# Alternating the two tokens of an output block over its partitions: x's columns reordered, stores from every other partition

## The chip, the cores and the metric

The kernel runs on one core of a Trainium2 chip. The metric is the device time of one execution in microseconds (us), and less is better. Before the change the median of three runs is 231.18 us (231.02 to 231.35).

## What is computed

The reference is a linear attention whose output goes through a feed-forward network with a multiplicative gate. There are 8 batches, 8 heads, 576 tokens in each batch and 64 channels in each head; the network goes from 512 to 1024 to 512 channels. q, k, v, the weights and the output are float32.

```python
def _attn_ref(q, k, v):
    q_s = exp(q - max(q, over channels));  q_s = q_s / (sum(q_s, over channels) + 1e-09)
    k_s = exp(k - max(k, over tokens));    k_s = k_s / (sum(k_s, over tokens) + 1e-09)
    kv = einsum('bhsd,bhse->bhde', k_s, v)
    return einsum('bhsd,bhde->bhse', q_s, kv)

def _moe_ref(x, w1, w2, w3, w_out):
    a = x @ w1
    b = x @ w2
    h = a * b @ w3
    return h @ w_out

x = attn_out.transpose(0, 2, 1, 3).reshape(B * S, H * D)     # 4608 tokens x 512
out = _moe_ref(x, w1, w2, w3, w_out)
```

## The kernel before, in words

**Weights.** `w3` and `w_out` are multiplied once, at the start, into one matrix `W3O`, so that the network is a gate (two products with `w1` and `w2`, multiplied element by element into `ab`) and one product of `ab` with `W3O`.

**Tokens.** A batch is one chunk. A token s of a batch is written as s = 9p + j, with p from 0 to 63 and j from 0 to 8. The attention of a batch gives x transposed, with channels on partitions and tokens along the columns. The tile `x` (128 partitions, 4 blocks of channels, 512 columns, f16) holds the tokens with j from 0 to 7, in the order j first, p second, so the 64 tokens of one j are neighbours. The tokens with j = 8 of all batches go into a tile of their own, `xtail`, which is a ninth chunk at the end.

**From attention to x.** The matmuls `xm` (line 704) write the attention's output into PSUM; `xs` evicts it with a factor into `x`, on ACT (line 369) or DVE (line 371). Batches 0 and 1 are split: their first 256 columns (`xs.b.0.i`) and their second 256 columns (`xs.b.1.i`) are evicted apart, each eviction writing two of the four blocks of channels, i = 0 the blocks 0 and 2, i = 1 the blocks 1 and 3. In the other batches an eviction writes all 512 columns of one block. There are 32 such evictions, 26 on ACT and 6 on DVE.

**The gate.** In batches 0 to 5, `up` (line 850) multiplies x with `w2` and `w1` into the PSUM tiles `pab`; the first product is evicted as `bsb`, and DVE multiplies the second with it into `ab` (line 865). In a split batch one `up` has 8 matmuls: two groups of 128 gate channels, in each the four blocks of channels of 256 columns. Chunks 6 to 8 make their gate from sums of x's halves of 256 columns (lines 921 and 938).

**The output.** In chunks 0 and 1, `down` (line 872) gives a block of 128 tokens and all 512 output channels. In chunks 2 to 8 seven products (line 1028) give blocks with 2 times 128 tokens and 256 output channels. A block's partitions are 128 neighbouring columns of x: partitions 0 to 63 hold the tokens of one j, partitions 64 to 127 those of the next j. Each block of chunks 0 to 7 is stored by two DMAs from SP's queue, one for each half of the partitions (lines 912 and 1071). That makes 64 issues, 56 that read `osb` and 8 that read `k` and `v`, input buffers that chunk 7 uses again. The ninth chunk is stored from all 128 partitions (lines 1058 and 1064).

**The order.** Each engine's order is written out by hand in the table `ORDER` at the top of the file. SP's queue holds the stores, most loads of q, k and v, and the transposing DMAs (line 679), which turn `en` (the softmax of q) into `qT`. The engines run in the order given and wait on semaphores; the waits are put in by the tile framework, from the regions of tiles that the instructions write and read.

The beginning of the first chunk, which the prediction speaks of, stands so in the table:

```python
... xm.0.0 pf.6.0 pf.6.1 xs.0.0.1 kmx.1.0 xs.0.0.0 xm.0.1 xs.0.1.0 xs.0.1.1 up.1.0.0.0 bs.0.0.0 xt.0 ...
```

So on PE the first product of the gate (`up.1.0.0.0`, which reads columns 0 to 255 of x) follows the matmuls `xm.0.1`, whose eviction writes columns 256 to 511; after it come the matmuls `xt` for the ninth chunk.

Of the kernel before, what the change touches and what calls it, by code (L numbers as in the profile page):

```python
# [265 lines left out]
def kernel(  # L266
# [12 lines left out]
    B, H, S, D = q.shape  # L279
# [7 lines left out]
    HALF = P // G  # L287
    HH = H // G
    NHP = HH // 2
    NJ = S // HALF  # L290
# [4 lines left out]
    SC = 2.0 ** 4.5  # L295
# [29 lines left out]
    st = {}  # L325
# [41 lines left out]
    def scale(eng, out, in_, by):  # L367
        if eng == "ACT":
            nc.scalar.mul(out=out, in_=in_, mul=by)
        else:  # L370
            engine[eng].tensor_scalar_mul(out=out, in0=in_, scalar1=by)
# [148 lines left out]
    def attention(b):  # L520
# [119 lines left out]
        def qeps(p, eng):  # L640
            rr = st["qr", b][:, :, slice(*PARTS[p])]
            if eng == "ACT":
                nc.scalar.activation(out=rr, in_=rr, func=AF.Identity, bias=epst[:, 0:1])
            else:
                return [dve.tensor_scalar_add(out=rr, in0=rr, scalar1=EPS)]
# [40 lines left out]
        def xtile():  # L686
            if ("x", b) not in st:
                st["x", b] = work.tile([P, N_CT, MAIN], F16, tag="x", name="x", bufs=NX)
            return st["x", b]
# [18 lines left out]
                            rhs=toks(i, hp, gg, j0, j1), start=True, stop=True)  # L708

        def xs(name, i, dst, eng):  # L710
            scale(eng, dst(), st[(*name, i)], SC)

        A0 = LEAD[min(b, 2)]

# [19 lines left out]
        for p in parts:  # L734
            n = (PARTS[p][1] - PARTS[p][0]) * HH * D
# [6 lines left out]
              lambda eng, p=p: qeps(p, eng), [("qsm", b, p)])  # L742
# [24 lines left out]
        if len(SUBS[b]) == 2:  # L767
            for h in range(2):
                name = ("xm", b, h)
                dst = lambda i, h=h: xtile()[:, i::2, h * 256:(h + 1) * 256]  # L770
                A(name, "PE", 0.22, lambda name=name, h=h: prod(name, [0, 1], 4 * h, 4 * h + 4, None),
                  kvs + qready(h) + free, takes=XRING(name), slots=2, slack=SLACK)
                for i in range(2):
                    A(("xs", b, h, i), moves(512), 0,
                      lambda eng, name=name, i=i, dst=dst: xs(name, i, lambda: dst(i), eng), [name],
# [3 lines left out]
        else:  # L779
            for hp in hps:  # L780
                name = ("xm", b, hp)
                A(name, "PE", 0.22, lambda name=name, hp=hp: prod(name, [hp], 0, NM, None),
                  kvs + qready(0) + qready(1) + free, takes=XRING(name), slots=2, slack=SLACK)
                for i in range(2):
                    A(("xs", b, hp, i), moves(512), 0,
                      lambda eng, name=name, i=i, hp=hp: xs(
                          name, i, lambda: xtile()[:, 2 * hp + i:2 * hp + i + 1, :], eng),
# [5 lines left out]
        for i in range(2):  # L793
            A(("xts", b, i), moves(128), 0,
              lambda eng, i=i: xs(("xt", b), i, lambda: xtail[:, i::2, b * HALF:(b + 1) * HALF], eng),
              [("xt", b)], gives=[("xt", b)])
# [39 lines left out]
    def chunk(c):  # L836
# [68 lines left out]
        def os2(tb, c0, c1, eng):  # L905
            st["osb", c, tb, c0] = obuf(c1 - c0)
            copy(eng, st["osb", c, tb, c0], st["po", c, tb, c0][:, 0:c1 - c0])

        def store(tb):
            for i in range(2):  # L910
                b, j = c, 2 * tb + i
                nc.sync.dma_start(
                    out=out[b * S:(b + 1) * S, :].rearrange("(p j) c -> p j c", j=NJ)[:, j, :],
                    in_=st["osb", c, tb][i * HALF:(i + 1) * HALF, :])

        def x_sum(i, eng):
            x0, x1 = [x()[:, 0:2, t:t + 256] for t in (0, 256)], [x()[:, 2:4, t:t + 256] for t in (0, 256)]
            b11, b12, b21, b22 = x0[0], x0[1], x1[0], x1[1]
            s = xsums(c)
            in0, in1 = {1: (b12, b11), 2: (b22, s[0]), 3: (b22, b12), 4: (b21, s[1])}[i]  # L920
            return [engine[eng].tensor_tensor(out=s[i - 1], in0=in0, in1=in1, op=ALU.subtract)]
# [79 lines left out]
        def sums_of(i, eng):  # L1001
            a = st["ab", c]
            a11, a12, a21, a22 = [a[:, 4 * f:4 * f + 4, 256 * t:256 * t + 256]
                                  for t in range(2) for f in range(2)]
            in0, in1, op = {1: (a21, a22, ALU.add), 2: (mine[0], a11, ALU.subtract),
                            3: (a11, a21, ALU.subtract), 4: (a12, mine[1], ALU.subtract)}[i]
            return [engine[eng].tensor_tensor(out=mine[i - 1], in0=in0, in1=in1, op=op)]  # L1007
# [47 lines left out]
        def store_block(n, part=None):  # L1055
            t0, c0 = n // 10 - 1, (n % 10 - 1) * 256
            if part is not None:
                (nc.sync if part else nc.scalar).dma_start(
                    out=out.rearrange("(t p j) c -> p t j c", p=P, j=NJ)[
                        :, 2 * t0 + part, NM, c0:c0 + 256],  # L1060
                    in_=st["osb", c, n][:, 256 * part:256 * part + 256])
                return
            if c == B:
                nc.sync.dma_start(
                    out=out.rearrange("(t p j) c -> p t j c", p=P, j=NJ)[
                        :, 2 * t0:2 * t0 + 2, NM, c0:c0 + 256],
                    in_=st["osb", c, n].rearrange("p (t x) -> p t x", t=2))
                return
            for i in range(2):
                j = 4 * t0 + i  # L1070
                nc.sync.dma_start(
                    out=out[c * S:(c + 1) * S, :].rearrange("(p j) c -> p j c", j=NJ)[
                        :, j:j + 3:2, c0:c0 + 256],
                    in_=st["osb", c, n][i * HALF:(i + 1) * HALF, :].rearrange(
                        "p (t x) -> p t x", t=2))

        A = plan.add
        nf = len(SUBS[c])
# [7 lines left out]
        if c in UPS + UP1:  # L1086
# [15 lines left out]
            for i, needs in ((1, []), (2, [("xd", c, 1)]), (3, []), (4, [("xd", c, 2)])):  # L1102
                A(("xd", c, i), {"POOL": (1.06, True), "DVE": (0.39, True)}, 0,
                  lambda eng, i=i: x_sum(i, eng), needs + xn + held)
            for g in range(2):
                for one in kinds:
                    k = lambda i: ("vk", one, c, g, i)
                    p = lambda i: ("vp", one, c, g, i)
# [12 lines left out]
                    for n, needs, gives in (  # L1121
# [8 lines left out]
                        b = ("bs", c, sub, u)  # L1130
# [33 lines left out]
        if c in SEVEN:  # L1164
# [8 lines left out]
            for i, needs in ((3, lo), (1, lo + hi), (2, [("sa", c, 1)]), (4, [("sa", c, 2)])):  # L1173
                A(("sa", c, i), {"POOL": (1.9, True), "DVE": (0.69, True)}, 0,
                  lambda eng, i=i: sums_of(i, eng), needs + last)
# [39 lines left out]
        for sub in range(nf):  # L1215
            for tb in range(4):
# [18 lines left out]
                for c0, c1 in zip(cuts, cuts[1:]):  # L1235
# [4 lines left out]
                      lambda eng, tb=tb, c0=c0, c1=c1: os2(tb, c0, c1, eng), [("down", *it)] + gone,  # L1240
# [6 lines left out]
    def weight_sum(i, eng):  # L1247
        b11, b12, b21, b22 = [W3O[:, 4 * f:4 * f + 4, 256 * x:256 * x + 256]
                              for f in range(2) for x in range(2)]
        in0, in1 = {1: (b12, b11), 2: (b22, sums[0]), 3: (b22, b12), 4: (b21, sums[1])}[i]  # L1250
        return [engine[eng].tensor_tensor(out=sums[i - 1], in0=in0, in1=in1, op=ALU.subtract)]

    for i, needs in ((1, []), (2, [("sT", 1)]), (3, []), (4, [("sT", 2)])):
        plan.add(("sT", i), {"POOL": (1.9, True), "DVE": (0.69, True)}, 0,
                 lambda eng, i=i: weight_sum(i, eng),
# [48 lines left out]
```

## Time and profile before

| What | us |
|---|---|
| median of 3 runs | 231.18 (231.02 to 231.35) |
| the profiled execution's own time | 230.82 |
| its span, first to last instruction | 229.0 |
| PE busy | 221.0 (96% of the span) |
| DVE busy | 202.4 (88%) |
| ACT busy | 146.2 (64%) |
| POOL busy | 144.0 (63%) |

The profile shows one execution. In a row of an engine's timeline stand the start and the length in us, the engine, the line, the operation, the tiles as written <- read, the shapes, the number of instructions merged into the row, and in brackets how long the engine was idle before it and who ended that. Matmuls are pipelined, and a row of them reaches past the moment at which the next row's first matmul starts; the distance between two rows' starts tells what a group took. SP only issues DMAs.

### The profile page before, as it was taken

Reading aid. Unit: us, or ns where it says so; the run is one execution under the profiler, and the core shown is the slowest. Engines: PE = TensorE matmul, PEld = TensorE weight load, DVE = VectorE, ACT = ScalarE, POOL = GpSimd, SP = SyncE. Lnnn points to the kernel's source line nnn. Section 1 sums busy time; section 2 is a strip of 40 time slices with the busy share of each in tenths; the row PEclk is TensorE's granted clock in tenths of the full one; section 3 lists DMA queues with packets and bytes.
Section 4 is the critical chain, followed back from the end, with each engine's and each line's share of the span. In section 5 each row is a group of like instructions: output and inputs, shape, how many; then the busy total and the mean of one; then the engine's idle time right before and its main releaser. Section 6 shows DMA issues by size and latency. Waiting matters only on the chain.

```text
span 229.0 us, 5580 instructions
## 1 busy us (share of the span) xinstructions
PE 221.0 (96%) x2239; PEld 149.3 (65%) x2239; DVE 202.4 (88%) x313; ACT 146.2 (64%) x277; POOL 144.0 (63%) x93
## 2 busy tenths in 40 slices
PE   7889999999999999999999999999999999999993
PEld 2445658865857644345666665664788788888882
DVE  2996769989896999999999899899989999899982
ACT  1536855479963999959947988448568453344531
POOL 8233347919999997984895894643199335628200
PEclk9999999999999999999999999999999999999999
DMA  6999999999999889999792867972804430041437
GB/s 202 218 308 215 291 264 258 316 383 305 399 306 239 345 274 216 294 277 339 229 394 63 166 137 170 345 144 53 178 1 88 95 64 1 3 92 35 106 90 231
DMA packets 42201, 46.56 MB, mean 203 GB/s; under 512 B 17088, under 2 KB 29888, under 8 KB 42176
## 3 DMA queue, kind: packets, MB, share of 16 engines
q1 hardware_dynamic: 34496, 34.35, 53.8%
q0 software_dynamic: 7536, 11.73, 21.9%
q8 instruction: 17, 0.28, 0.5%
q10 hardware_dynamic: 144, 0.13, 0.2%
q14 instruction: 8, 0.07, 0.1%
HBM read 38.80 MB, written 9.44 MB: 211 GB/s over the span
## 4 chain that ended last, share of the span: by engine, by line
PE 73%; POOL 9%; DMA 9%; issue 4%; DVE 3%; ACT 1%; POOLq 0%; DVEq 0%
PE pab L850 27%; PE po L1028 16%; PE pg L938 9%; PE pab L938 7%; DMA w<-in_moe_w_dram 7%; PE po L500 4%; POOL k L554 3%; PE pab L1028 2%; POOL en L656 2%; DMA qT<-en 2%; PE pkv L579 2%; POOL q L624 2%; PE po L872 2%; PE xm L704 1%; PE w3t L488 1%
## 5 line engine op out<-in xcount | busy, mean ns | idle before, releaser
L850 PE MATMUL pab<-x,w1sb 128*128 128x256 f16 (+1 forms) x256 | 49.5, 326 | 0.2 <-DMA w1sb<-in_moe_w_dram 0.2
L850 PE MATMUL pab<-x,w2sb 128*128 128x256 f16 (+1 forms) x256 | 49.5, 326 | 0.0
L554 POOL TENSOR_TENSOR k<-k,cb 128x1152 f32<-128x1152 f32 x13 | 34.1, 2631 | 14.4 <-DVE w L1007 8.6
L850 PEld LDWEIGHTS <-w1sb 128*128 128x128 f16 x256 | 24.6, 98 | 14.9 <-DMA w1sb<-in_moe_w_dram 0.5
L850 PEld LDWEIGHTS <-w2sb 128*128 128x128 f16 x256 | 24.3, 98 | 15.1 <-issue 1.1
L865 DVE TENSOR_TENSOR ab<-pab,bsb 128x512 f16<-128x512 f32 x48 | 31.8, 676 | 1.9 <-ACT bsb L365 1.2
L624 POOL TENSOR_TENSOR q<-q,qm 128x1280 f32<-128x1280 f32 (+1 forms) x13 | 27.8, 2142 | 4.7 <-issue 2.3
L365 ACT CAST bsb<-pab 128x512 f16<-128x512 f32 x37 | 21.7, 586 | 12.6 <-PE pab L850 12.1
L656 POOL TENSOR_TENSOR en<-eq,qr 128x1024 f16<-128x1024 f16 (+1 forms) x12 | 25.4, 2123 | 6.0 <-ACT bsb L365 5.0
L619 DVE TENSOR_REDUCE qm<-q 128x20 f32<-128x1280 f32 (+1 forms) x16 | 21.3, 1339 | 3.5 <-DMA q<-in_q_dram 3.5
L637 DVE TENSOR_REDUCE qr<-eq 128x20 f32<-128x1280 f16 (+1 forms) x16 | 21.4, 1340 | 1.1 <-ACT eq L632 1.0
L632 ACT ACTIVATE eq<-q 128x1280 f16<-128x1280 f32 (+1 forms) x16 | 18.6, 1168 | 5.4 <-DVE q L624 3.8
L1028 PEld LDWEIGHTS <-w 128*128 128x128 f16 x192 | 18.6, 98 | 4.1 <-issue 0.4
L531 DVE TRANSPOSE_TENSOR_REDUCE kt<-k 128x72 f32<-128x2304 f32 x8 | 20.6, 2570 | 0.3 <-DMA k<-in_k_dram 0.3
L365 ACT COPY q<-pg 128x512 f32<-128x512 f32 x19 | 10.9, 586 | 13.9 <-PE pg L938 7.7
L1028 PEld LDWEIGHTS <-ab 128*128 128x128 f16 x168 | 16.4, 98 | 3.5 <-issue 0.2
L562 ACT ACTIVATE ek<-k 128x1152 f16<-128x1152 f32 x16 | 18.4, 1166 | 0.0
L1028 PE MATMUL po<-w 128*128 128x256 f16 x144 | 18.0, 273 | 0.0
L1007 POOL TENSOR_TENSOR w<-ab 128x1024 f16<-128x1024 f16 x5 | 10.6, 2126 | 9.7 <-DVE ab L993 3.7
L500 PE MATMUL po<-wosb,w3T 128*128 128x512 f16 x64 | 15.3, 379 | 0.6 <-DMA wosb<-in_moe_w_out_dram 0.5
L872 PE MATMUL po<-W3O,ab 128*128 128x512 f16 x64 | 15.1, 379 | 0.0
L365 ACT CAST v<-v 128x1152 f16<-128x1152 f32 x12 | 13.6, 1156 | 1.2 <-DMA v<-in_v_dram 1.1
(145 smaller groups left out, 426.0 us busy)
## 6 DMA issues: line engine op xcount, KB each, us to landing
out_dram<-osb SPq DMA_DIRECT2D x56, 128.0 KB, 2.5
q<-in_q_dram SPq DMA_DIRECT2D x5, 1152.0 KB, 8.2
v<-in_v_dram SPq DMA_DIRECT2D x5, 1152.0 KB, 7.1
k<-in_k_dram SPq DMA_DIRECT2D x4, 1152.0 KB, 9.5
k<-in_k_dram POOLq DMA_DIRECT2D x3, 1152.0 KB, 14.1
v<-in_v_dram POOLq DMA_DIRECT2D x1, 1152.0 KB, 13.6
q<-in_q_dram SPq DMA_DIRECT2D x2, 576.0 KB, 5.7
k<-in_k_dram SPq DMA_DIRECT2D x2, 576.0 KB, 5.7
```

Source lines behind the costliest of these rows:

```text
L365: return [(nc.scalar.copy if eng == "ACT" else engine[eng].tensor_copy)(out=out, in_=in_)]
L500: nc.tensor.matmul(st["pf", ft], lhsT=st["w3T", ft][:, gt, :], rhs=wosb[:, gt, :], start=(gt == 0), stop=(gt == N_FT - 1))
L531: dve.tensor_reduce(out=st["kt", b].rearrange("p h j e -> p (h j e)"), in_=kb.rearrange("p h j (e c) -> p (h j e) c", c=QD), axis=AX.X, op ...
L554: return [engine[eng].tensor_tensor(out=kb[:, two(hp), :, :], in0=kb[:, two(hp), :, :], in1=st["cb", b][:, two(hp), None, :].broadcast_to( ...
L619: dve.tensor_reduce(out=st["qm", b][:, :, j], in_=qb[:, :, j, :], axis=AX.X, op=ALU.max)
L624: return [engine[eng].tensor_tensor(out=qb[:, :, j, :], in0=qb[:, :, j, :], in1=st["qm", b][:, :, j, None].broadcast_to([P, HH, n, D]), op ...
L637: dve.tensor_reduce(out=st["qr", b][:, :, slice(*PARTS[p])], in_=st["eq", b, p], axis=AX.X, op=ALU.add)
L656: return [engine[eng].tensor_tensor(out=st["en", b][:, j, :, :].rearrange("p j h d -> p h j d"), in0=st["eq", b, p], in1=st["qr", b][:, :, ...
L850: nc.tensor.matmul(st["p", one, c, sub, u][:, a * (t1 - t0):(a + 1) * (t1 - t0)], lhsT=w[:, ct, fb * P:(fb + 1) * P], rhs=x()[:, ct, t0:t1 ...
L865: dve.tensor_tensor(out=st["ab", c][:, nf * u:nf * u + nf, t0:t1], in0=cut(st["p", 0, c, sub, u]), in1=cut(st["bsb", c, sub, u]), op=ALU.mult)
L938: nc.tensor.matmul(st["pg", one, c, g, bank][:, a * 256:a * 256 + 256], lhsT=t[:, c0 + ct, f:f + P], rhs=r[:, r0 + ct, t0:t0 + 256], start ...
L1028: nc.tensor.matmul(to, lhsT=t[:, f0 + ft, t0 + tb * P:t0 + tb * P + P], rhs=r[:, g0 + ft, c0:c0 + 256], start=fresh and (tb == 0 or wide_) ...
```

## The change

`xs` writes the evicted columns in another order. In each run of 256 columns, which are four values of j, let j = 2z + t within the run; the column of token (p, j) was 128z + 64t + p and is now 128t + 2p + z. An output block (128 columns, one t) then holds the tokens of two values of j alternately, z = 0 on the even partitions and z = 1 on the odd ones. The two stores of a block take the even and the odd partitions, 64 each, where they took the lower and the upper half; in chunks 2 to 7 the two rows of the output that one partition's data goes to are now neighbours (j and j + 1), where they were j and j + 2. The `xtail` tile and the ninth chunk's stores are left as they are. Each store moves as many bytes as before, and no instruction is added or removed.

```diff
         def xs(name, i, dst, eng):
-            scale(eng, dst(), st[(*name, i)], SC)
+            to, ps = dst(), st[(*name, i)]
+            if name[0] == "xm":
+                if ps.shape[1] == 1:
+                    to = to[:, 0, :].rearrange("p (a t c z) -> p a z t c", t=2, z=2, c=HALF)
+                    ps = ps[:, 0, :].rearrange("p (a z t c) -> p a z t c", t=2, z=2, c=HALF)
+                else:
+                    to = to.rearrange("p a (t c z) -> p a z t c", z=2, c=HALF)
+                    ps = ps.rearrange("p a (z t c) -> p a z t c", z=2, c=HALF)
+            scale(eng, to, ps, SC)
...
         def store(tb):
-            for i in range(2):
-                b, j = c, 2 * tb + i
+            for z in range(2):
+                j = tb // 2 * 4 + tb % 2 + 2 * z
                 nc.sync.dma_start(
-                    out=out[b * S:(b + 1) * S, :].rearrange("(p j) c -> p j c", j=NJ)[:, j, :],
-                    in_=st["osb", c, tb][i * HALF:(i + 1) * HALF, :])
+                    out=out[c * S:(c + 1) * S, :].rearrange("(p j) c -> p j c", j=NJ)[:, j, :],
+                    in_=st["osb", c, tb][z::2, :])
...
-            for i in range(2):
-                j = 4 * t0 + i
+            for z in range(2):
+                j = 4 * t0 + 2 * z
                 nc.sync.dma_start(
                     out=out[c * S:(c + 1) * S, :].rearrange("(p j) c -> p j c", j=NJ)[
-                        :, j:j + 3:2, c0:c0 + 256],
-                    in_=st["osb", c, n][i * HALF:(i + 1) * HALF, :].rearrange(
-                        "p (t x) -> p t x", t=2))
+                        :, j:j + 2, c0:c0 + 256],
+                    in_=st["osb", c, n][z::2, :].rearrange("p (t x) -> p t x", t=2))
```

Below is what the built programs show at the beginning of the first chunk. On PE before, from the last matmul of `xm.0.1` over the first product of the gate (8 weight loads and 8 matmuls, the first pair shown) to the matmuls `xt`; a name in brackets is the semaphore of an engine, or of a DMA queue, that the instruction waits for:

```order
L704 MATMUL xm<-qT,kv_479 64x256
L850 LDWEIGHTS w2sb [waits DMASW3_49]
L850 MATMUL pab<-x,w2sb 128x256
...
L704 LDWEIGHTS kv_479
L704 MATMUL xt<-qT,kv_479 64x64 [waits Activation_49]
L704 LDWEIGHTS kv_479
L704 MATMUL xt<-qT,kv_479 64x64
L704 LDWEIGHTS kv_479
L704 MATMUL xt<-qT,kv_479 64x64 [waits DVE_49]
```

The same place on PE in the changed kernel, the first three pairs of the gate's product shown (line 858 is line 850 before):

```order
L704 MATMUL xm<-qT,kv_479 64x256
L858 LDWEIGHTS w2sb [waits DMASW3_49]
L858 MATMUL pab<-x,w2sb 128x256
L858 LDWEIGHTS w2sb
L858 MATMUL pab<-x,w2sb 128x256 [waits Activation_49]
L858 LDWEIGHTS w2sb
L858 MATMUL pab<-x,w2sb 128x256 [waits DVE_49]
...
L704 LDWEIGHTS kv_479
L704 MATMUL xt<-qT,kv_479 64x64 [waits PE_49]
```

The instructions stand in the same order, but the waits for ACT and for DVE have moved ahead, from the first and third matmul of `xt` to the second and third matmul of the gate's first product. They wait for the same two counts as before, those of the evictions `xs.0.1.0` on ACT and `xs.0.1.1` on DVE. This is the only place in the program at which an instruction waits for something else than before.

On DVE, at the eviction `xs.0.1.1` before:

```order
L531 TENSOR_REDUCE kt<-k_1_76 128x72 [waits DMASW2_49]
L371 TENSOR_SCALAR x<-xm 128x2x256 [waits PE_49]
L619 TENSOR_REDUCE qm<-q_1_78 128x4x4 [waits DMASW4_49]
L537 TENSOR_REDUCE mx<-kt 128x8 [waits DVE_49]
L371 TENSOR_SCALAR W3O<-po 128x512
```

The same in the changed kernel:

```order
L531 TENSOR_REDUCE kt<-k_1_76 128x72 [waits DMASW2_49]
L371 TENSOR_SCALAR x<-xm 128x2x2x128 [waits PE_49]
L619 TENSOR_REDUCE qm<-q_1_78 128x4x4 [waits DMASW4_49]
L537 TENSOR_REDUCE mx<-kt 128x8 [waits DVE_49]
L371 TENSOR_SCALAR W3O<-po 128x512
```

The eviction keeps its place, its wait and its 512 elements; its output pattern has one more dimension (two blocks, two values of z, 128 columns at a distance of two). The other evictions of x, on DVE and on ACT, change in the same way, and nothing else on these engines, on POOL or in SP's queue differs in place or in what it waits for.

## The prediction

> **What bounds the kernel now.** I read the page's busy times and the chain of waits first, then PE's waits, then the timelines around the places that the change touches.
>
> ```profile
> span 229.0 us, 5580 instructions
> PE 221.0 (96%) x2239; PEld 149.3 (65%) x2239; DVE 202.4 (88%) x313; ACT 146.2 (64%) x277; POOL 144.0 (63%) x93
> PE 73%; POOL 9%; DMA 9%; issue 4%; DVE 3%; ACT 1%; POOLq 0%; DVEq 0%
> ...
> PE xm L704 <- DMA qT<-en: 0.4, 1, 0.4
> PE pab L850 <- DMA w1sb<-in_moe_w_dram: 0.2, 1, 0.2
> PE po L1028 <- ACT x L369: 0.2, 1, 0.2
> ```
>
> PE is busy for 221.0 of 229.0 us, and these three rows are all the waits that its matmuls have behind the weights' folding. So nearly every us by which PE's stream is held up is paid, unless it meets one of these waits, and hardly anything can be won on another engine or on a DMA. The chain goes through POOL and a transposing DMA up to 73 us, and from there through PE to the end, with one eviction of x in it:
>
> ```profile
> 68.20 4.95 DMA qT<-en
> 73.15 0.14 issue
> 73.28 0.41 PE xm L704 x4
> ...
> 181.36 0.56 ACT x L369
> 181.92 0.04 issue
> 181.96 1.03 PE po L1028 x8
> ```
>
> **The change, part by part.** It touches three things: a wait on PE, the write pattern of 32 evictions, and the source pattern of 64 stores.
>
> *The wait.* PE and the two evictions at the first chunk:
>
> ```profile
> 33.57 1.05 PE L850 MATMUL pab<-x,w2sb 128*128 128x256 f16 x8
> 34.55 0.25 PE L704 MATMUL xt<-qT,kv 64*64 64x64 f16 x8
> ...
> 35.67 1.04 PE L850 MATMUL pab<-x,w2sb 128*128 128x256 f16 x8
> 36.54 1.04 PE L850 MATMUL pab<-x,w1sb 128*128 128x256 f16 x8
> 33.68 0.60 ACT L369 ACTIVATE x<-xm 128x512 f16<-128x512 f32 x1 [1.07 <-PE xm L704]
> 33.72 0.69 DVE L371 TENSOR_SCALAR x<-xm 128x512 f16<-128x512 f32 x1 [0.28 <-PE xm L704]
> ```
>
> Before, the gate's first product starts at 33.57, beside the evictions of `xm.0.1`, since it reads only the other half of the columns. In the changed program its second matmul waits for ACT and its third for DVE. The reason is in the pattern: the eviction with i = 0 writes blocks 0 and 2 with a stride, and taken as one run from its first to its last element it also covers block 1's first half, which the second matmul reads; the one with i = 1 covers block 2's first half, which the third reads. The data don't ask for it. A group of 8 matmuls takes 36.54 - 35.67 = 0.87 us, 0.109 each, so the third starts at 33.57 + 0.22 = 33.79 now. It will start when DVE ends, 33.72 + 0.69 = 34.41, and 0.04 later (the issue row at 181.92, PE behind an eviction of x): 34.45. ACT ends at 34.28, which is earlier. The stall is 34.45 - 33.79 = **0.66 us**. Everything on PE behind it, `xt` first, is late by that; `xt`'s own waits for the same two engines were met at 34.55 and are gone, which at most gives the hundredths that they may have cost.
>
> *What takes it back.* The next places at which PE waits for something that doesn't depend on PE:
>
> ```profile
> 44.40 1.04 PE L850 MATMUL pab<-x,w2sb 128*128 128x256 f16 x8
> 45.63 1.05 PE L850 MATMUL pab<-x,w1sb 128*128 128x256 f16 x8 [0.19 <-DMA w1sb<-in_moe_w_dram]
> 47.39 1.89 PE L872 MATMUL po<-W3O,ab 128*128 128x512 f16 x8
> ...
> 49.31 0.69 DVE L365 COPY osb<-po 128x512 f32<-128x512 f32 x1 [0.69 <-PE po L872]
> 49.92 1.35 DVE L554 TENSOR_TENSOR k<-k,cb 128x1152 f32<-128x1152 f32 x1
> 51.35 2.64 POOL L554 TENSOR_TENSOR k<-k,cb 128x1152 f32<-128x1152 f32 x1 [5.00 <-DVE k L554]
> 53.95 6.51 POOL L624 TENSOR_TENSOR q<-q,qm 128x1280 f32<-128x1280 f32 x3
> 60.40 1.15 POOL L365 CAST v<-v 128x1152 f16<-128x1152 f32 x1
> 61.67 6.50 POOL L656 TENSOR_TENSOR en<-eq,qr 128x1280 f16<-128x1280 f16 x3
> ```
>
> The group at 45.63 would have started at 44.40 + 0.87 = 45.27, had its weights been there. It lost 0.36; the weights' load was issued long before 33 us and doesn't move. With 0.66 of delay the group is ready at 45.93 and waits no more: 0.66 - 0.36 = **0.30 us** is left. This delay goes on along two ways. PE itself is late by 0.30. And DVE's copy at 49.31 waits for PE's product of 47.39, DVE's subtraction at 49.92 stands behind it in DVE's order, and POOL's at 51.35 waits 5.00 us for that; from there POOL's queue has no gap to the `en` that ends at 61.67 + 6.50 = 68.17, so the transposing DMA is issued 0.30 later as well.
>
> ```profile
> 71.83 1.04 PE L850 MATMUL pab<-x,w1sb 128*128 128x256 f16 x8
> 73.28 0.41 PE L704 MATMUL xm<-qT,kv 64*64 64x512 f16 x4 [0.41 <-DMA qT<-en]
> ...
> 60.00:70.00 10.00, 10.00 (x157) 6.80 (x156) 9.90 (x16) 6.82 (x14) 9.87 (x6) 1.00 1.02 330
> qT<-en SPq DMA_TRANSPOSE x13, 3.8
> ```
>
> The two ways meet at 73.28. Before, PE's last group ends at 72.87 and PE waits 0.41 for `qT`. PE's own 0.30 fits into that. So what counts is by how much `qT` lands later: by 0.30 if its transfer takes its 4.95 again, by nothing if the transfer was held by the DMA engines' queue rather than by its issue. The queue is full (a DMA share of 1.02 between 60 and 70 us), and 4.95 is 1.15 over the median of 3.8, which would cover the 0.30; but SP issues in order, and the loads that compete move back with the transposes. I take **0.2 us** between the ends 0 and 0.30, nearer the upper since most of what stands around the transfer moves with it. From 73.28 the chain is PE's alone, so the 0.2 stays to the end. Price of the wait: +0.2, with bounds 0 (all absorbed) and 0.66 (nothing absorbed).
>
> *The evictions.* 26 on ACT and 6 on DVE now write f16 at a distance of two elements. The number of elements stays. No row of this kernel has such a write.
>
> ```profile
> L369 ACT ACTIVATE x<-xm x18: 577/597/632, 31.5 to 181.8; 128x512 f16<-128x512 f32 x18
> L371 DVE TENSOR_SCALAR x<-xm x4: 679/686/692, 33.7 to 182.1; 128x512 f16<-128x512 f32 x4
> L365 ACT COPY osb<-po x10: 583/586/592, 52.2 to 180.5; 128x512 f32<-128x512 f32 x10
> ```
>
> ACT takes 597 ns for 512 f16 elements side by side and 586 ns for 512 f32: twice the bytes at the same time, so the price goes by elements and not by how closely they lie. DVE's 686 ns for 512 is likewise over 1 ns an element. I take 0. The upper end is that a scattered element costs double, +0.6 us an eviction. PE covers most of them with other work; not covered are the one of 33.7 us and the pair before PE's wait at 181.96, so at that end the kernel loses up to 0.6 + 2 x 0.6 = 1.8 us. The lower end is 0.
>
> The Trainium skill (SBUF — State Buffer, "Door 1: The DMA port swizzle") says that an engine's strided access keeps its full rate while at least two accesses fall into one 16-byte line; f16 at a distance of two has four, so by this rule the price is 0 too. No run here shows it yet.
>
> *The stores.*
>
> ```profile
> L1071 SPq DMA_DIRECT2D out_dram<-osb x40: 595/603/652, 123.7 to 211.6; - x40
> L912 SPq DMA_DIRECT2D out_dram<-osb x16: 502/582/1927, 51.3 to 113.1; - x16
> L1058 SPq DMA_DIRECT2D out_dram<-v x1: 344/344/344, 225.7 to 225.7; - x1
> out_dram<-osb SPq DMA_DIRECT2D x56, 128.0 KB, 2.5
> out_dram<-v SPq DMA_DIRECT2D x2, 256.0 KB, 2.6
> ```
>
> 64 stores keep their bytes, their pieces and their place in SP's queue. An issue takes 582 to 603 ns; I bound it by the shortest and longest rows, 344 and 1927, and take no change. Behind the stores in SP's order stand loads and transposes; the only one of these on the chain is that of 68.20 us, and the four stores ahead of it are issued by 55.1 us, so even the long issue would be hidden there. The landing may get shorter: a store of 256 KB from all 128 partitions lands in 2.6 us, one of 128 KB from 64 neighbouring partitions in 2.5, so 64 neighbours move about half as fast. No wait of a computing engine names an output store, so I cost this at nothing; its cover is the ring of four `osb` buffers. At the program's end the last stores are the ninth chunk's, which don't change.
>
> The Trainium skill (same page and section) gives this as a rule: partitions 0 to 63 reach 8 of the 16 ports between SBUF and the DMA engines, and only a range with both halves reaches all. The two rows agree with it. By the rule the changed stores would be faster, and a kernel bound by stores would win; that is the third rival below.
>
> **The sum.** 0.66 - 0.36 - 0.10 = +0.2 us. Against the profiled execution's 230.82 (1.82 more than its span) that is 231.0; the median of the runs, 231.18, stands 0.36 above that execution, so I forecast 231.18 + 0.2 = **231.4 us**, less than 0.2% (0.46 us) above, which is about what a measurement of this kernel can tell from no change.
>
> **The rivals.**
> - *The stall is paid in full: slower.* PE's 0.66 is taken back only where the weights at 45.63 and `qT` at 73.28 come at the same time as before. If the loads at these two places come later by chance or because the DMA engines' order shifts, 0.5 to 0.7 stays: 231.7 to 231.9. It decides from 0.46 us that are not absorbed. For it: PE has no other gap of that size up to 181 us. Against it: the load of w1 was issued before the stall.
> - *The scattered writes are slower.* From +0.15 us an eviction the three uncovered ones and the stall at 33.7 together pass 0.46; at double price 231.18 + 0.2 + 1.8 = 233.2. Against it: 597 and 586 ns for f16 and f32.
> - *The stores give the DMA engines time back.* Four stores of 51.3 to 55.1 us lie ahead of the loads that `qT` waits behind. If these are done sooner, `qT` lands sooner, but PE is ready only at 72.87 + 0.30, so at most about 0.1 is won against 73.28: 231.1. To be faster by over 0.2% more than this is needed, for instance 0.2 at the end of the program.
> - *Nothing happens:* the added waits are met when PE comes to them. Against it: DVE ends its eviction 0.62 us after PE's third matmul starts.
>
> **How the numbers follow.** Forecast (0 to 0.45 left): 0.50, all of it within 0.2%. Full stall: 0.20, slower. Slower writes: 0.12, slower. Stores: 0.13, of which 0.10 faster, with something besides, and 0.03 within. Nothing: 0.05, within. So faster 0.10, within 0.2% 0.58, slower 0.32. The range must leave out no more than 0.2: below, the stores' case is cut at 230.7, which leaves out about 0.07; above, 232.2 takes in the full stall and the writes at half the upper end, and leaves out about 0.07. The likeliest case alone is 231.2 to 231.6.
>
> **What will show it.** In the changed kernel PE should wait for DVE's x inside the first gate product near 34.4 us, and start `xt` about 0.66 later; the wait for w1 at 45.63 should be gone, and that for `qT` at 73.28 small. The 32 evictions should keep 597 and 686 ns, and the stores of chunks 2 to 7 should land in less than 2.5 us with no engine gaining. I am wrong if a gap appears on PE behind 73 us, if an eviction of x is longer by over 0.1 us, or if an issue of a store on SP grows so that a transpose comes late.

## The result and the profile after

The changed kernel takes 231.59 us (median of 17 runs, 231.26 to 231.81), the kernel before 231.01 us beside it (17 runs, 230.67 to 231.40). The ratio is 1.0022, with a 95% interval of 1.0015 to 1.0029: slower by 0.58 us. The ratios here and below are taken over all runs of both kernels, so they can differ by up to 0.1% from the quotient of two medians. The profiled execution of the changed kernel took 231.59 us, its span is 229.8 us against 229.0.

All waits of PE's matmuls behind the folding of the weights, after (us in total, times, longest); of before three such rows stand in the prediction:

```profile
PE pab L858 <- ACT x L369: 0.6, 1, 0.6
PE xm L704 <- DMA qT<-en: 0.5, 1, 0.5
...
PE po L1036 <- ACT x L369: 0.3, 1, 0.3
```

The first is the moved wait. The wait for w1 is gone, the one for `qT` is there as before, and the last is longer by 0.1. The chain of waits now goes through the added wait, and then, as before, through the transposing DMA:

```profile
33.90 0.73 ACT x L369
34.63 0.04 issue
34.67 0.93 PE pab L858 x7
...
68.77 4.94 DMA qT<-en
73.71 0.14 issue
73.85 0.41 PE xm L704 x4
```

The evictions of x by tile and form (ns as minimum, median and maximum, then first and last start), after:

```profile
L369 ACT ACTIVATE x<-xm x18: 725/744/779, 31.7 to 182.7; 128x512 f16<-128x512 f32 x18
...
L369 ACT ACTIVATE x<-po x8: 738/747/775, 96.2 to 182.1; 128x512 f16<-128x512 f32 x8
L371 DVE TENSOR_SCALAR x<-xm x4: 711/726/731, 33.9 to 183.0; 128x512 f16<-128x512 f32 x4
...
L371 DVE TENSOR_SCALAR x<-po x2: 728/728/728, 139.3 to 182.4; 128x512 f16<-128x512 f32 x2
```

On ACT an eviction went from 597 to 744 ns (+0.15 us), on DVE from 686 to 726 (+0.04). The stores' issue on SP, after, in the same form:

```profile
L1079 SPq DMA_DIRECT2D out_dram<-osb x40: 600/604/720, 124.9 to 212.5; - x40
```

The DMA part of the profile after: packets, MB and share of the 16 engines' time of the queue that the stores are in, and the median landing of the stores in us:

```profile
q1 hardware_dynamic: 34496, 34.35, 49.8%
...
out_dram<-osb SPq DMA_DIRECT2D x56, 128.0 KB, 2.2
```

The queue's row before:

```profile
q1 hardware_dynamic: 34496, 34.35, 53.8%
```

An issue takes what it took (604 ns, before 603). A store of 128 KB lands in 2.2 us instead of 2.5, and the same 34.35 MB occupy the DMA engines for 4 points less. This is what the Trainium skill says (SBUF — State Buffer, "Door 1: The DMA port swizzle") of partitions spread over both halves.

**Where PE loses the time.** PE's timeline after, at the places of the prediction (start, length, and in brackets the idle time ahead):

```profile
33.78 0.28 PE L858 MATMUL pab<-x,w2sb 128*128 128x256 f16 x1
34.67 0.93 PE L858 MATMUL pab<-x,w2sb 128*128 128x256 f16 x7 [0.61 <-ACT x L369]
35.53 0.26 PE L704 MATMUL xt<-qT,kv 64*64 64x64 f16 x8
...
36.60 1.04 PE L858 MATMUL pab<-x,w2sb 128*128 128x256 f16 x8
...
46.20 1.04 PE L858 MATMUL pab<-x,w1sb 128*128 128x256 f16 x8
47.08 1.04 PE L858 MATMUL pab<-x,w2sb 128*128 128x256 f16 x8
...
73.85 0.41 PE L704 MATMUL xm<-qT,kv 64*64 64x512 f16 x4 [0.53 <-DMA qT<-en]
...
81.59 1.03 PE L858 MATMUL pab<-x,w2sb 128*128 128x512 f16 x4
82.65 1.67 PE L880 MATMUL po<-W3O,ab 128*128 128x512 f16 x7
...
182.91 1.03 PE L1036 MATMUL po<-W3O,ab 128*128 128x256 f16 x8 [0.31 <-ACT x L369]
```

and before, where the prediction didn't show it:

```profile
81.03 1.03 PE L850 MATMUL pab<-x,w2sb 128*128 128x512 f16 x4
81.89 1.89 PE L872 MATMUL po<-W3O,ab 128*128 128x512 f16 x8
```

The gate's first product starts at 33.78 (before 33.57): this execution is 0.21 late already, from the load of the first weights, and that has nothing to do with the change. Counted from there, the product of 36.60 (before 35.67) is 0.72 late, that of 47.08 (46.52) 0.35, `xm` at 73.85 (73.28) 0.36, the output's product at 82.65 (81.89) 0.55 and that of 182.91 (181.96) 0.74; the end of the span is late by 0.8 - 0.21 = 0.59. This agrees with the 0.58 us between the medians. So there are three losses (the wait, one near 82 us, one near 182 us), one return at the w1 wait, and 0.15 that come back between 182 us and the end. Of these, 0.06 come back at once: the group at 182.91 takes 0.87 us to the next group's start, where it took 0.93 before. The rest lies behind the last store, further below.

The second loss is ACT's. Its timeline before:

```profile
75.94 1.09 ACT L369 ACTIVATE x<-xm 128x512 f16<-128x512 f32 x2
...
81.18 0.58 ACT L365 COPY osb<-po 128x512 f32<-128x512 f32 x1
```

and after:

```profile
76.50 1.36 ACT L369 ACTIVATE x<-xm 128x512 f16<-128x512 f32 x2
...
82.01 0.58 ACT L365 COPY osb<-po 128x512 f32<-128x512 f32 x1
```

Two evictions took 1.09 us and take 1.36. From there to the copy of `osb` ACT has no gap in either. The copy empties the PSUM tile that PE's next `po` product writes. Before, it ended at 81.76, and PE came to the product at 81.89, 81.89 - 81.03 = 0.86 us after its last group's start: a reserve of 0.13 us. Now PE would come at 81.59 + 0.86 = 82.45, but the copy ends at 82.59 and PE starts at 82.65: about 0.2 us are lost.

### The profile page after: what moved, and what is told of

It is laid out like the page before. It is cut to its first block, busy times and chain, and to the rows that moved or that the text cites. A ratio compares the mean times of both kernels' runs of the same rounds, so it can differ in the third digit from the quotient of the medians.

```text
span 229.8 us, 5580 instructions
## 1 busy us (share of the span) xinstructions
PE 220.6 (96%) x2239; PEld 149.2 (65%) x2239; DVE 202.6 (88%) x313; ACT 149.1 (65%) x277; POOL 144.1 (63%) x93
## 3 DMA queue, kind: packets, MB, share of 16 engines
q1 hardware_dynamic: 34496, 34.35, 49.8%
## 4 chain that ended last, share of the span: by engine, by line
PE 82%; DMA 9%; POOL 4%; DVE 2%; ACT 1%; issue 1%; DVEq 0%; POOLq 0%
PE pab L858 33%; PE po L1036 16%; PE pg L946 9%; PE pab L946 7%; DMA w<-in_moe_w_dram 7%; PE po L880 5%; PE po L500 4%; PE pab L1036 2%; PE pkv L579 2%; DMA qT<-en 2%; POOL en L656 2%; PE xm L704 1%; PE w3t L488 1%; POOL w L449 1%; ACT x L369 1%
## 5 line engine op out<-in xcount | busy, mean ns | idle before, releaser
L369 ACT ACTIVATE x<-xm 128x512 f16<-128x512 f32 x18 | 12.7, 748 | 3.6 <-PE xm L704 3.6
```

## The experiments

A table from PE's timelines comes first, since most of the verdicts rest on it; it has all runs but the one in which the matmuls themselves reorder the columns: times in us between five landmarks, which are the start of the gate's first product, the start of its second `w2` product, `xm` behind the `qT` wait, the output's product near 82 us, the one near 182 us behind ACT's x, and the end of the span. For before they are 33.57, 35.67, 73.28, 81.89, 181.96 and 229.0. Where a kernel ran in two groups of runs, both values stand.

| kernel | first product to second | to `xm` | to 82 us | to 182 us | to the end | ratio [95%] |
|---|---|---|---|---|---|---|
| before | 2.10 | 37.61 | 8.61 | 100.07 | 47.0 | 1 |
| after | 2.82, 2.81 | 37.25, 37.14 | 8.80, 8.80 | 100.26, 100.26 | 46.9, 46.9 | 1.0022 [1.0015, 1.0029], 1.0017 [1.0005, 1.0029] |
| stores only | 2.05, 2.05 | 37.22, 37.43 | 8.61, 8.61 | 100.30, 100.26 | 46.9, 47.0 | 0.9984 [0.9973, 0.9996], 0.9993 [0.9978, 1.0009] |
| order only | 2.82, 2.82 | 37.20, 37.16 | 8.80, 8.79 | 100.45, 100.31 | 47.0, 47.0 | 1.0015 [1.0000, 1.0031], 1.0028 [1.0018, 1.0038] |
| wait only | 2.73, 2.73 | 36.77, 37.18 | 9.33, 8.61 | 100.09, 100.05 | 47.1, 47.2 | 1.0006 [0.9992, 1.0020], 1.0013 [0.9999, 1.0026] |
| batches 0 and 1 | 2.82 | 37.19 | 8.61 | 100.06 | 47.1 | 1.0018 [1.0006, 1.0030] |
| batches 2 to 7 | 2.08 | 37.52 | 8.79 | 100.28 | 47.0 | 0.9996 [0.9985, 1.0007] |
| read at a distance, wait stays | 2.70 | 37.19 | 8.61 | 100.17 | 47.0 | 1.0004 [0.9990, 1.0017] |
| read at a distance, no wait | 2.05 | 38.01 | 8.61 | 100.08 | 47.0 | 0.9999 [0.9988, 1.0010] |

**The stores alone.** The two store functions of the change, with x in its old order:

```diff
...
-            for i in range(2):
-                j = 4 * t0 + i
+            for z in range(2):
+                j = 4 * t0 + 2 * z
...
-                        :, j:j + 3:2, c0:c0 + 256],
-                    in_=st["osb", c, n][i * HALF:(i + 1) * HALF, :].rearrange(
+                        :, j:j + 2, c0:c0 + 256],
+                    in_=st["osb", c, n][z::2, :].rearrange("p (t x) -> p t x", t=2))
```

> Before with the new stores alone: x keeps its old order, so the rows of the output land in other places than the reference's; the work is the same. Theory (the loss is made of the earlier wait on PE and of evictions of x that are 0.15 us longer on ACT; the stores are hidden): ratio to before 1.000, within 0.1%, with the 128 KB stores landing in 2.2 us where they took 2.5. Rival 1 (stores that are done sooner give the DMA engines time back and win): 0.998 to 0.999. Rival 2 (part of the loss is the stores'): 1.001 or more.

Measured 230.78 us against 231.13. It was run again in another group, to see whether the gain holds:

> The new stores alone, with x's old order (rows land in other places than the reference's), a second time, since 0.9984 with an interval of 0.9973 to 0.9996 was more than the 0.1 us at the program's end explains. Theory: 0.9990 to 1.000, the 0.1 us being the only gain. Rival (the stores win 0.3 us or more somewhere): 0.998 to 0.9988 again.

Measured 230.71 against 230.99, with an interval that holds 1. The landing is 2.2 and 2.3 us, evictions and waits are as before, and the first column of the table is that of before. So on the whole the stores lose nothing. The first group lies below the range that was expected, where the first rival put it, and shows a gain; the second doesn't confirm it. The traces have some 0.1 us of a gain, behind the last store, which is shown further below. The lead of both runs at `xm` (37.22 and 37.43 against 37.61) is not the stores': it arises where PE waits for w1 near 45.6 us, and the kernel before issues its first store at 51.3.

**x's order alone.** The change to `xs`, with the old stores:

```diff
-            scale(eng, dst(), st[(*name, i)], SC)
+            to, ps = dst(), st[(*name, i)]
+            if name[0] == "xm":
...
+            scale(eng, to, ps, SC)
```

> x's new order with the old stores (rows land in other places than the reference's; the work is the same). Theory: everything that was lost is here, ratio 1.002 (231.5), stores landing in 2.5 us. Rival 1 (the stores win something in the full change, which hides a larger loss): 1.003 or more. Rival 2 (the stores are part of the loss): 1.001 or less.

Measured 231.72 us against 231.13, and in the second group 231.68 against 230.99:

> x's new order with the old stores (rows land in other places than the reference's), a second time, beside the others: the first run gave 1.0015 with an interval of 1.0000 to 1.0031. Theory: at or above the full change, 1.002 to 1.003, since it has the wait and the longer evictions and not the 0.1 us that the stores win at the end. Rival (the stores are part of the loss): 1.001.

All of the loss is in this part. Its profile has the added wait and the long evictions; x's tile in the second group:

```profile
L369 ACT ACTIVATE x<-xm x18: 717/745/783, 31.8 to 182.7; 128x512 f16<-128x512 f32 x18
```

The stores land in 2.5 and 2.7 us there, as before or later. So neither the wait nor the long evictions come from the stores.

**The wait alone.** The kernel before, with the second and third matmul of `up.1.0.0.0` made to wait for the two evictions:

```diff
...
+                        if (c, sub, u, one, a) == (0, 0, 0, 1, 0) and ct in (1, 2):
+                            link(d, st["evict", ("xm", 0, 1), ct - 1])
```

> Before, with the two waits alone put on PE: the second and third matmul of the first gate product wait for the ACT and DVE evictions of the other half; x's order, evictions and stores as before. Theory: PE stalls 0.66 us near 33.8 us (evictions keep 597 and 686 ns), 0.36 of it is taken back at the w1 wait of 45.6 us and some at the next waits, 0.1 to 0.3 us is left: ratio 1.0005 to 1.0015. Rival 1 (the wait is the whole loss): 1.002. Rival 2 (the wait is all absorbed, the evictions are the loss): 1.000.

Measured 231.19 us against 231.13. PE's timeline:

```profile
33.36 0.28 PE L849 MATMUL pab<-x,w2sb 128*128 128x256 f16 x1
34.12 0.97 PE L849 MATMUL pab<-x,w2sb 128*128 128x256 f16 x7 [0.47 <-ACT x L369]
...
36.09 1.04 PE L849 MATMUL pab<-x,w2sb 128*128 128x256 f16 x8
...
82.19 1.89 PE L873 MATMUL po<-W3O,ab 128*128 128x512 f16 x8 [0.56 <-ACT osb L365]
```

The stall is 2.73 - 2.10 = 0.63 us, against 0.72 in the changed kernel: 0.09 of the changed kernel's stall belongs to ACT's longer eviction. The wait of 0.56 at 82.19 is another matter, which the second group doesn't have: ACT's cast of v came late there, since a load had landed late.

```profile
78.86 1.16 ACT L365 CAST v<-v 128x1152 f16<-128x1152 f32 x1 [0.70 <-DMA v<-in_v_dram]
```

> The two earlier waits alone, a second time, beside the others: the first run gave 1.0006 with an interval of 0.9992 to 1.002. Theory: 1.0005 to 1.0015. Rival (the wait is the whole loss of 0.2%): 1.002.

Measured 231.50 against 230.99. From the first landmark to `xm` behind `qT` this run takes 2.73 + 37.18 = 39.91 us, before 39.71: 0.20 of the 0.63 is left. The first run takes 2.73 + 36.77 = 39.50 us, which is 0.21 less than before, so one execution doesn't settle how much is left. The medians are 0.06 and 0.51 us above the kernel before, and both intervals hold 1: a loss by the wait alone is not shown by them, nor do they exclude that it is the whole 0.2%.

What PE gets back at w1 differs between executions, too. The load that it waits for at 45.63 in the kernel before is issued by POOL at 33.68, behind a load of q, and lands 11.9 us later:

```profile
33.68 0.74 POOL L449 DMA_DIRECT2D w1sb<-in_moe_w_dram  x1 [0.61 <-DMA q<-in_q_dram]
```

There the group of 45.63 starts 1.23 us behind the group ahead of it, and without a wait it would be 0.87: 0.36 us are lost. In the other kernels that don't have the added wait the same distance is 0.87 and 1.06 us (stores alone), 1.22 (batches 2 to 7), 0.87 (reordering in the matmuls) and 1.40 (reading side, without the wait). So an execution without the added wait loses 0 to 0.53 us at w1, and every execution with it loses nothing there.

**One half of the batches, then the other.** The change of `xs` and of the stores in batches 2 to 7 only, and in batches 0 and 1 only:

```diff
-            if name[0] == "xm":
+            if name[0] == "xm" and b >= 2:
...
```

> The change in batches 2 to 7 alone; batches 0 and 1, whose chunks are split, keep x's old order and the old stores, and the program has no wait that before doesn't have. Theory: no stall at 33.8 us, evictions of batches 2 to 7 at 750 ns on ACT; ACT is later by 0.3 us where two stand in a row, PE is held by that near 82 us (a product that waits for ACT's copy of an output block) and near 182 us: 0.2 to 0.35 us, ratio 1.001 to 1.0015. Rival 1 (the wait is the whole loss): 1.000. Rival 2 (the evictions are the whole loss): 1.002.

Measured 231.12 us against 231.09.

```diff
-            if name[0] == "xm":
+            if name[0] == "xm" and b < 2:
...
```

> The change in batches 0 and 1 alone, with the earlier wait; batches 2 to 7 as before. Theory: the stall is there at 0.79 us (0.66, and the eviction longer by up to 0.15), and 0.1 to 0.4 us of it is left behind 73 us: ratio 1.0005 to 1.0015, and together with the run of batches 2 to 7 alone it gives the full change's loss. Rival 1 (the wait is the whole loss): 1.002. Rival 2 (late evictions are the whole loss): 1.000.

Measured 231.45 against 231.09. In the table the two runs share out the losses: the stall (2.82) and the return behind it lie in batches 0 and 1, and the loss near 82 us (8.79) and the longer wait near 182 us in batches 2 to 7. PE's timeline in the run of batches 2 to 7:

```profile
82.06 1.89 PE L880 MATMUL po<-W3O,ab 128*128 128x512 f16 x8
...
182.34 1.03 PE L1036 MATMUL po<-W3O,ab 128*128 128x256 f16 x8 [0.32 <-ACT x L369]
```

and ACT's:

```profile
75.92 1.35 ACT L369 ACTIVATE x<-xm 128x512 f16<-128x512 f32 x2
...
81.43 0.58 ACT L365 COPY osb<-po 128x512 f32<-128x512 f32 x1
```

ACT ends its copy at 82.01, and PE starts 0.05 later; so the 0.19 us near 82 us come from the two long evictions, without the added wait. The medians say something else. Batches 2 to 7 alone lose nothing, where a ratio of 1.001 to 1.0015 was expected, and batches 0 and 1 alone lose 0.36 us (1.0018), more than the 1.0015 expected: both lie where the rival put them by which the wait is the whole loss. That the faster stores of batches 2 to 7 make up for the late evictions would fit, but it is not shown.

**The reordering in the matmuls.** The evictions and the wait are left as before; instead the `xm` matmuls write their PSUM columns in the new order, at a distance of two:

```diff
...
-                            st[(*name, i)][gg * D:(gg + 1) * D, a, :].rearrange(
-                                "p (j c) -> p j c", c=HALF),
+                            o.rearrange("p (h t c z) -> p h z t c", t=2, z=2, c=HALF),
```

> The new order and the new stores, but the columns are reordered where the attention's matmuls write PSUM (every other f32 column), so that the evictions of x write neighbours again; the program then has none of the two earlier waits. Theory: evictions back at 597 and 686 ns, no stall at 33.8 us, stores landing in 2.2 us; if the matmuls keep their pace the ratio is 1.000. Rival (a matmul that writes every other column of PSUM is slower): the 32 groups of matmuls before evictions, 0.34 us each for 8 half-size or 4 full-size matmuls, take up to twice as long, and PE loses 0.1 to 0.34 us for each pair, ratio 1.005 to 1.02.

Measured 233.19 us against 231.13, ratio 1.0092 [1.0064, 1.0120]. The last group of these matmuls, before:

```profile
180.88 0.63 PE L704 MATMUL po<-qT,kv 64*64 64x512 f16 x4
181.11 0.61 PE L704 MATMUL xm<-qT,kv 64*64 64x512 f16 x4
```

and with PE writing every other column:

```profile
183.53 0.84 PE L711 MATMUL po<-qT,kv 64*64 64x512 f16 x4
183.92 0.88 PE L711 MATMUL xm<-qT,kv 64*64 64x512 f16 x4
```

Four matmuls take 0.39 us from start to start instead of 0.23. The work of reordering is dearest here, since PE is what the kernel waits for. The Trainium skill (SBUF — State Buffer, "Door 1: The DMA port swizzle") says that PSUM's lines have 8 bytes and that a matmul is slowed by any pattern that isn't contiguous; these rows agree.

**The reordering on the reading side, with the wait.** The eviction reads PSUM at a distance of 128 f32 and writes its f16 side by side, in a pattern of as many dimensions as in the change:

```diff
...
-                    to = to.rearrange("p a (t c z) -> p a z t c", z=2, c=HALF)
-                    ps = ps.rearrange("p a (z t c) -> p a z t c", z=2, c=HALF)
+                    to = to.rearrange("p a (t c z) -> p a t c z", z=2, c=HALF)
+                    ps = ps.rearrange("p a (z t c) -> p a t c z", z=2, c=HALF)
```

> The new order and stores, with the eviction walking its output in order and its PSUM input at a distance (128 columns for the two values of z) instead. The two earlier waits on PE stay in the program. Theory: what costs the 0.15 us is the scattered f16 write, so ACT's evictions are back near 597 ns, unless PSUM is read more slowly that way; the stall alone is left, ratio 1.0005 to 1.0015. Rival (the extra dimensions of the pattern cost, not the distance): 740 ns or more, ratio 1.002.

Measured 231.22 us against 231.09, a ratio of 1.0004 with an interval that holds 1; the changed kernel beside it has 1.0017. The two intervals overlap, so the medians suggest that the long evictions cost something, but don't show it. The evictions are as short as before, as the view of x's tile shows:

```profile
L369 ACT ACTIVATE x<-xm x18: 577/597/632, 32.0 to 182.6; 128x512 f16<-128x512 f32 x18
...
L371 DVE TENSOR_SCALAR x<-xm x4: 678/686/692, 34.2 to 182.9; 128x512 f16<-128x512 f32 x4
```

and the wait is still there in PE's timeline:

```profile
34.79 0.95 PE L858 MATMUL pab<-x,w2sb 128*128 128x256 f16 x7 [0.47 <-ACT x L369]
```

So what costs ACT 0.15 us is the write of every other f16, not the number of dimensions and not the reading order. And the wait does not come from the distance of two: the written elements are here the same runs of 256 columns as before the change. Here the framework put it in for a contiguous output that is only written down in more dimensions.

**The reordering on the reading side, without the wait.** The same, but in the split batches 0 and 1 the output stays the plain rows of the kernel before. In the other batches, whose lines are left out here, it is still contiguous and written down in more dimensions; no wait came of that there.

```diff
...
-                    to = to.rearrange("p a (t c z) -> p a z t c", z=2, c=HALF)
-                    ps = ps.rearrange("p a (z t c) -> p a z t c", z=2, c=HALF)
+                    ps = ps.rearrange("p a (z n) -> p a n z", z=2)
```

> The whole change with the eviction's PSUM input walked at a distance (as in the read-side run, where ACT kept 597 ns) and its output given as the plain rows of 256 columns, so that the program has none of the two earlier waits. Theory (wait and scattered write are the whole loss; the new stores alone shorten the program's last landings by 0.1 us): no stall near 33.8 us, evictions at 597 and 686 ns, stores of 128 KB landing in 2.2 us, from the last store's issue to the span's end 2.87 us instead of 2.95; ratio 0.9985 to 1.000. Rival (reading PSUM at a distance or the new order costs somewhere else): 1.001 or more.

Measured 230.97 us against 230.99. It computes what the changed kernel computes, with the new stores, and the loss is gone. Its profile has neither the wait nor long evictions; PE runs through the first product:

```profile
33.71 1.05 PE L857 MATMUL pab<-x,w2sb 128*128 128x256 f16 x8
34.68 0.26 PE L704 MATMUL xt<-qT,kv 64*64 64x64 f16 x8
```

The 38.01 in its row of the table comes from weights that landed late in this execution: PE's groups at 44.79 (w2) and 46.19 (w1) start 1.17 and 1.40 us behind the group ahead, instead of 0.87. The version doesn't beat the kernel before: with an interval of 0.9988 to 1.0010 no gain is shown.

**The changed kernel again**, beside the two halves of the batches:

> The full change on the same chip as the three others, for comparison: ratio 1.002, stall of 0.79 us near 33.8 us, ACT's evictions of x at 750 ns.

Measured 231.41 us against 231.09; its times between the landmarks agree with those of the first profile within 0.11 us.

## Why the prediction was right, and where not

The forecast was 231.4 us, 0.2 above the kernel before; the time is 231.59, and 0.58 above the kernel before in the same runs. That lies within the range, but just past the 0.46 us up to which the prediction called the time the same. The forecast was made of the wait alone. By the traces a term that it put at nothing, the evictions, cost 0.41 us, and that the time still came so near to it is in part luck: 0.15 came back behind 182 us, for which the sum had no term. The range holds the time since it was made wide for two rivals, the full stall and the slower writes.

- **The wait: right.** It appeared where the prediction put it, inside the first gate product. Alone it stalls PE by 0.63 us (0.66 forecast), with ACT's longer eviction by 0.72. In the changed kernel it was ACT's eviction and not DVE's that ended it, since ACT became slower by 0.15 and DVE by 0.04. The reason given, that the strided pattern is taken as one run, was incomplete: a contiguous output in more dimensions gets the same wait.
- **What takes it back: right at w1 in this execution, wrong at `qT`.** 0.37 came back by 47.08 us (0.36 forecast), and the way over DVE and POOL to the transposing DMA moved as described. The close agreement at w1 is luck in part, since an execution without the wait loses anything from 0 to 0.53 us there; and the load was not issued long before 33 us but at 33.68. What held is that it stands behind another load and not behind PE. The 0.10 that was taken off at `qT` didn't come: the transfer took 4.94 us (before 4.95), began 0.57 later, of which 0.21 is the late start, and PE waited for it again, 0.53 us. 0.36 was left in the changed kernel (0.24 in its second profile), and 0.20 and -0.21 with the wait alone, where 0.2 had been taken. Without the wait the time to `xm` runs from 39.27 to 40.06 us by the table, so how much of the wait is left on average stays open.
- **The evictions: the step that failed.** "I take 0" was wrong on ACT: 0.15 us an eviction. The argument from f16 and f32 side by side taking the same time says nothing of elements that don't lie side by side. The Trainium skill's rule of two accesses in one 16-byte line (SBUF — State Buffer, "Door 1: The DMA port swizzle") would make this write free, since four fall into a line; the measured 744 against 597 ns decides against it for ACT's write. PE paid 0.09 in the stall, 0.19 near 82 us and 0.13 at the wait near 182 us (0.18 to 0.31), 0.41 together. The middle one wasn't among the uncovered evictions that the prediction named; there the cover was thinner, 0.13 us, than two evictions' growth of 0.27. Near 182 us it named a pair, but ACT's rows of before show that only the first of the two ends ahead of PE's start at 181.96:

```profile
181.31 0.60 ACT L369 ACTIVATE x<-po 128x512 f16<-128x512 f32 x1
181.80 0.59 ACT L369 ACTIVATE x<-xm 128x512 f16<-128x512 f32 x1
```

The price of +0.15 us is that of the second rival (0.12), at its threshold: "from +0.15 us an eviction" the sum passes 0.46. That three times 0.15 comes near the measured 0.41 is luck, since the places were not the three that it counted.
- **The stores: priced at nothing, and nearly that.** Landing and DMA share improved as foreseen, and the median issue of a store stayed (one of the 64, a store of k, took 1.67 us). At the program's end the last store is issued at 225.73 before and at 226.60 after, and the span ends 3.31 and 3.21 us later. In the traces of all eight runs with the new stores in chunks 2 to 7 this time is 3.18 to 3.23 us, and in the six with the old ones 3.28 to 3.44: about 0.1 us is won there. The prediction held that these stores don't change; they don't, but those just ahead of them in the queue do, which is the likely reason. SP's last row before:

```profile
225.73 0.34 SPq L1058 DMA_DIRECT2D out_dram<-v  x1
```

and after:

```profile
226.60 0.34 SPq L1066 DMA_DIRECT2D out_dram<-v  x1
```

- **The sum, made again** from the changed kernel's row of the table against that of before: +0.72 (the stall) - 0.36 (the way to `xm`) + 0.19 (near 82 us) + 0.19 (to 182 us) - 0.15 (to the end) = +0.59 us.

Two things stay open. Whether the stores win more than the 0.1 us at the end: the medians of the stores alone are 0.35 and 0.28 below the kernel before, but the second interval reaches 1, and the version without wait and long evictions doesn't repeat it. The full change (0.58 and 0.32 us above before) against x's order alone (0.59 and 0.69) would fit some gain, but these intervals overlap. And the exact shares of the wait and of the evictions in the 0.58: by the traces they are 0.2 to 0.3 and 0.4, less what the stores give back; by the medians of the two halves of the batches nearly all of it lies in batches 0 and 1. The intervals are too wide to say it better. What is shown is the whole: without the wait and the long evictions, and with the new stores, the loss is gone.

## What to carry to other kernels

When a store pattern asks for another order of columns, do the reordering where an engine reads PSUM and leave its output plain rows; here that cost nothing, while scattering the output cost 0.15 us an eviction on ACT and a wait that the data don't ask for, and scattering PE's own output cost 0.9% of the kernel. Look at where a pattern change puts waits before looking at the DMA it improves, and price an access pattern for which no row exists with both ends kept open. A wait that takes back a delay in one profile can be shorter or missing in the next, so look at several before subtracting it. An engine that is busy for 64% of the span can still set the pace wherever its reserve is 0.13 us.

## What the runs showed that was not expected

**A store that holds up DVE.** The prediction said that the ring of four `osb` buffers covers the stores. At one place it doesn't quite. With the stores alone, DVE:

```profile
155.54 0.69 DVE L1052 TENSOR_TENSOR osb<-po,kept 128x512 f32<-128x512 f32 x1 [0.54 <-PE pab L850]
```

PE is named, but what ends just before is a store from this ring: issued at 151.18 behind two transposing DMAs and a load of v, it lands at 155.46 in the trace, 4.3 us later instead of the usual 2.2. In the second run of the stores alone the landing is 155.39 and DVE starts at 155.47, and before it is 155.11 and 155.19: 0.08 us each time. By 163.5 us PE waits for DVE, and some 0.2 us are lost, which is the 100.30 and 100.26 of the table. The landing here is 3.8 us after the issue in the kernel before, 4.1 with x's order alone, both with the old stores, and 3.8 with the new ones in the version without the wait. So it is slow with either stores, and the 0.4 us more with the stores alone is not shown to come from them; what makes it stays open.

**The start differs between executions.** The gate's first product starts between 33.36 and 34.32 us in the profiles of the table, not ordered by kernel, as the first weights land earlier or later. That is more than the effect of the change, and the reason that only times counted from a landmark, or medians of a dozen runs and more, could separate the parts.
